# A fused recurrence, MLP and MoE kernel: the triangular products of a superchunk are issued at the end of the one before

## The chip, the cores and the metric

The kernel runs on one core of a Trainium2 chip. The number that counts is the time of one execution in device microseconds (us). Each value of an input is random and in float32; the whole program is one launch.

## The reference

Three layers run one after the other. The first is a recurrence over 768 steps with a 40 x 40 state for each of 4 batches and 8 heads; the second is an MLP with a squared ReLU on the 3072 resulting tokens; the third sends every token to one of 8 experts.

```python
for t in range(S):                                  # B, H, S, D = 4, 8, 768, 40
    y[:, :, t] = einsum('bhd,bhde->bhe', rt, state)
    Sa = einsum('bhde,bhe->bhd', state, at)
    state = state * wt[:, :, None, :] - einsum('bhd,bhe->bhde', Sa, bt) + einsum('bhd,bhe->bhde', vt, kt)
...
x = y, as (3072 tokens) x (8 heads * 40)
h = x @ w_in                                        # 320 -> 2048
x = (max(h, 0) ** 2) @ w_out                        # 2048 -> 320
...
expert = argmax(x @ w_gate)                         # 8 experts, capacity 768 each
y = max(x_e @ w1[e], 0) @ w2[e]                     # 320 -> 1024 -> 320
out = gate_w * y[expert]
```

## The kernel before

**The recurrence.** The 768 steps are cut into NS = 12 superchunks of 64 steps, each of NC = 2 chunks of 32. Within a superchunk the steps are coupled by triangular matrices, one of 32 x 32 for every chunk, head and batch. For superchunk s three methods make and use them. `lower(s, c)`, called for both chunks, issues 64 small matmuls `pa` of the scaled inputs `kb` (in the trace `kb_d`) and `a`, copies one half of the product by ACT into `ab` (two equal copies of it), masks the other half on DVE into `am`, and transposes that into `a` (the name `ak` in the code). `invert(s)` transposes `ab` into `al` on DVE and then inverts all the triangles at once on POOL, by 31 pairs of a multiplication (`tmp`) and a subtraction (`solve_tl`), which both stand at the helper's line L291. `inverted(s)` waits for the last of them, transposes the inverse on DVE (`solve_tf`, L221) and puts it together in `tt` (ACT L224, DVE L225). The solve of the superchunk's first chunk (`psa` on PE, then `sa` on ACT, L332) reads `tt`.

**The rest.** `scale(s)` scales the inputs by running products of the decay (the scans `rq_r` and `rq_q` over `w_d`), `decay(s)` multiplies `a` by the decay (DVE L350), and `step` ends a chunk by the update of the state `zv` (L308); the next superchunk begins with the output `y` (DVE L390), its transposition on PE (`pt`, L456), the decay of `zv` (DVE L350) and the transposition of `zv` (`pz`). The MLP works on the tokens of the preceding superchunk: `pl` products, ReLU and square on ACT and DVE (`g`, L660, split into `gh` and `gl`), `acc` products. Its weights come as doubles and are cut into two float parts at the start: a load on ACT's queue (L514), `Abs` on ACT (L519), four bit operations on DVE (L520 to L523), the high part on ACT (L554 for w_in, into `wi_hi`; L411 for w_out, into `woh`) and the low part by a subtraction, which is on POOL (L528) or on DVE (L530, `lo`). The w_out pieces are `ao0` to `ao15`; the w_in pieces are `a0_0`, `a0_1`, `a0_2` and so on, of which `a0_2` is put into the buffer of `a0_0` (tag "relu", two buffers). `wogl` (L412) are small subtractions for the router.

**What sets the order.** PE's matmuls run in the order in which the program is written (`mm`), and the instructions of an inversion on POOL are chained in their order as well. All else is ordered by a scheduler for each engine, which goes by the program's order, by priorities (higher for s < 2) and by its own estimate of the times. Each engine then runs its list strictly in order. A superchunk is written as seven slots for its first chunk and five for its second, each followed by some pieces of the MLP:

```python
parts = slot_a, slot_b, slot_c, slot_d, slot_e, slot_f, slot_g
if c == 1:
    parts = slot_a, slot_b, slot_d, slot_f, slot_g
```

`slot_a` holds `out` (y) and `right`, `slot_b` the solve, `slot_c` `lower` and `invert` of the next superchunk, `slot_g` the `step`, and in the second chunk `inverted` of the next superchunk behind it.

Of the kernel before, what the change touches and what calls it, by code (L numbers as in the profile page):

```python
# [72 lines left out]
class Rwkv:  # L73
# [101 lines left out]
    def lower(self, s, c):  # L175

        nc = self.nc
        kb, a = self.kb, self.a[s % 2][:, c]
        if c == 0:
            self.ab = self.tile([128, C, 2, NC, H], f"solve.ab{s}", 2)  # L180
        pa = self.psum(f"pa{s}_{c}").rearrange("p (h k s) -> p h k s", h=H, k=2)
        t0 = c * C
        for h, b, i, lane, ty, j in heads():
            rows = BY_COL[j]
            self.mm(pa[lane, h], lhsT=a[rows, j, i], rhs=kb[rows, :, i, t0:t0 + C], start=True, stop=True)
        for u in range(2):
            nc.scalar.copy(self.ab[:, :, u, c, :], pa[:, :, 1, :].rearrange("p h s -> p s h"))
        am = self.tile([128, H, C], f"am.{s}_{c}", 1)
        nc.vector.tensor_tensor(out=am, in0=pa[:, :, 0, :], in1=self.c["mlow"][:, None, :].to_broadcast([128, H, C]),
                                op=ALU.mult)  # L190
        for j in range(2):
            ak = a[BY_STEP[j], j].rearrange("p (h y) t -> p y h t", y=2)
            nc.vector.transpose(out=ak[:, 0], in_=am[BY_STEP[j]])  # L193
            nc.scalar.copy(ak[:, 1], ak[:, 0])

    def invert(self, s):

        nc = self.nc
        al = self.tile([128, C, C], f"solve.al{s}", 2)
        nc.vector.transpose(out=al.rearrange("p s t -> p (s t)"), in_=self.ab.rearrange("p s u c h -> p (s u c h)"))  # L200
        tl = self.tile([128, C, C // 2], f"solve.tl{s}", 2)
# [14 lines left out]
    def inverted(self, s):  # L216

        nc, tl = self.nc, self.tl
        tf = self.tile([128, C, 2, NC, H], f"solve.tf{s}", 2)
# [578 lines left out]
class Moe:  # L798
# [188 lines left out]
    def early(self, rw):  # L987
# [34 lines left out]
        op = [rw.tile([128, 8, 128], f"{t}.op{i}", 2 - i // 2, dt=F32R) for i, t in enumerate(("solve", "solve", "rq16"))]  # L1022
# [332 lines left out]
def tile_rwkv__mlp__moe(ctx, tc, wd, kb, ad, rv, wl, tok, vt, nat, w_in, w_out, w_gate, w1, w2, cap, cst1, cst2, cst3, out):  # L1355
# [9 lines left out]
    with ExitStack() as ph:  # L1365
# [53 lines left out]
        for s in range(NS):  # L1419
# [3 lines left out]
            for c in range(NC):  # L1423
# [7 lines left out]
                def slot_a():  # L1431
                    nonlocal y
                    if s == 0 and c == 0:
                        rw.inverted(0)
                    if last is not None:
                        y = rw.out(*last)
# [13 lines left out]
                def slot_c():  # L1450
                    if s > 1:
                        pieces.append(ml.bursts(s - 1, xs.pop(s - 1)))
                    if more:
                        rw.lower(s + 1, 0)
                        rw.lower(s + 1, 1)
                        rw.invert(s + 1)
# [21 lines left out]
                def slot_g():  # L1478
                    rw.step(s, c, 0)
                    rw.step(s, c, 1)  # L1480
                    if c == 1 and more:
                        rw.inverted(s + 1)

# [137 lines left out]
```

## Time and profile before

| | |
|---|---|
| three runs | 1124.78, 1127.44 and 1131.85 us; median 1127.44 us |
| the profiled execution | 1123.14 us, of which the trace's span is 1121.4 us |
| PE busy | 912.5 us, 81% of the span |
| DVE busy | 851.1 us, 76% |
| ACT busy | 573.1 us, 51% |
| POOL busy | 501.8 us, 45% |

The span falls into three parts. Up to about 226 us the weights are converted beside superchunks 0 and 1, and PE is often idle. From there to about 721 us superchunks 2 to 10 and the MLP run side by side, some 60 us for each. Then follow the last superchunk, the remaining MLP and the experts. A row of the timeline gives the start, the duration, the engine, the line, the operation with what it writes and reads, and in brackets how long the engine was idle before it and which instruction it waited for.

### The profile page before, as it was taken

To read this page: it belongs to the slowest core of one execution; us is meant where nothing else is said; L and a number is where in the kernel's file an instruction comes from. 1 tells how busy PE (TensorE), PEld (TensorE's weight loads), DVE (VectorE), ACT (ScalarE), POOL (GpSimd) and SP (SyncE) were. 2 spreads that over 40 slices of the span, in tenths; PEclk is the share of its full clock that TensorE was granted. 3 is DMA by queue.
4 is the path that set the end of the run, shared out by engine and by line. 5 is a ranking of instruction groups with operands and counts; after the bars stand their busy time and mean duration, and the time that the engine had idled before them with its cause. 6 is when DMAs were issued, how large, how long until landed. Compare 5 with 4: busy or idle time off the path is not lost.

```text
span 1121.4 us, 38788 instructions
## 1 busy us (share of the span) xinstructions
PE 912.5 (81%) x15962; PEld 858.4 (77%) x15962; DVE 851.1 (76%) x1807; ACT 573.1 (51%) x1570; POOL 501.8 (45%) x866
## 2 busy tenths in 40 slices
PE   1645347788798989897979889899899999999992
PEld 1535247687687878796978888899799989999992
DVE  8969887688778788777877888765777967878860
ACT  2425335454454544545545454555474667767750
POOL 4782852828282837465563828270010132223220
PEclk9999998888898989798998889899999998999997
DMA  8823534844353535353434444343195576767720
GB/s 219 251 81 110 147 114 112 267 121 134 104 147 114 151 105 168 90 155 116 135 110 129 133 127 144 91 136 104 39 321 146 163 219 189 229 199 231 216 80 9
DMA packets 86112, 164.19 MB, mean 146 GB/s; under 512 B 15709, under 2 KB 46047, under 8 KB 84960
## 3 DMA queue, kind: packets, MB, share of 16 engines
q1 hardware_dynamic: 76848, 141.52, 43.4%
q10 hardware_dynamic: 6192, 11.06, 3.6%
q0 software_dynamic: 2880, 8.98, 2.4%
q8 instruction: 129, 2.11, 0.8%
q14 instruction: 63, 0.52, 0.2%
HBM read 137.34 MB, written 16.24 MB: 137 GB/s over the span
## 4 chain that ended last, share of the span: by engine, by line
PE 36%; POOL 22%; DVE 16%; issue 9%; DMA 9%; ACT 3%; SPq 1%; POOLq 0%; DVEq 0%; ACTq 0%
POOL tmp L291 11%; POOL solve_tl L291 11%; PE acc L633 8%; PE pl L449 8%; PE upl L449 6%; PE uacc L1143 6%; DMA xg<-x_dram,room 3%; DVE rq_r L126 2%; DMA out_dram<-uo,room 2%; DVE rq_q L139 2%; DVE zv L350 1%; PE pa L294 1%; PE ppq L294 1%; DMA raw<-in_w_in_dram 1%; PE pn L294 1%
## 5 line engine op out<-in xcount | busy, mean ns | idle before, releaser
L291 POOL TENSOR_TENSOR tmp<-solve_al,solve_tl 128x126 f32<-128x126 f32 (+22 forms) x372 | 205.9, 554 | 41.1 <-DVE a L193 12.9
L291 POOL TENSOR_TENSOR solve_tl<-solve_tl,tmp 128x126 f32<-128x126 f32 (+22 forms) x372 | 199.1, 535 | 29.1
L633 PE MATMUL acc<-woh,gh 128*128 128x328 f32 x384 | 130.5, 345 | 1.6 <-ACT x L686 1.6
L449 PE MATMUL pl<-x_hi,wi_hi 128*128 128x256 f32 x384 | 122.2, 318 | 10.0 <-DVE g L660 5.8
L633 PE MATMUL acc<-wol,gh 128*128 128x328 f32 x384 | 123.8, 328 | 0.0
L449 PE MATMUL pl<-x_lo,wi_hi 128*128 128x256 f32 x384 | 115.0, 300 | 7.2 <-DVE x_lo L464 7.2
L660 DVE TENSOR_TENSOR g<-pl,g 128x512 f32<-128x512 f32 x96 | 65.6, 684 | 66.2 <-ACT gh L659 65.9
L449 PE MATMUL pl<-x_hi,wi_lo 128*128 128x256 f32 x384 | 114.9, 299 | 0.0
L291 POOL MEMSET solve_tl<- 128x512 f32 x12 | 6.3, 526 | 214.8 <-DVE solve_al L200 199.1
L1221 POOL DMA_INDIRECT out_dram<-uo,room x30 | 34.3, 1144 | 150.6 <-DVE uo L1210 83.0
L655 ACT ACTIVATE g<-pl 128x512 f32<-128x512 f32 x96 | 57.4, 598 | 76.4 <-PE pl L449 75.2
L633 PE MATMUL acc<-woh,gl 128*128 128x328 f32 x384 | 93.1, 325 | 0.0
L1151 POOL DMA_INDIRECT xg<-x_dram,room x30 | 30.7, 1022 | 139.0 <-DVE room L983 61.4
L449 PEld LDWEIGHTS pl<-x_hi,wi_hi 128*128 128x128 f32 x384 | 78.8, 205 | 14.3 <-DVE g L660 5.9
L449 PEld LDWEIGHTS pl<-x_lo,wi_hi 128*128 128x128 f32 x384 | 79.5, 207 | 7.5 <-DVE x_lo L464 7.5
L1143 PE MATMUL uacc<-w2h,hh 128*128 128x320 f32 x240 | 76.8, 320 | 10.1 <-DVE uo L1210 8.5
L633 PEld LDWEIGHTS acc<-woh,gh 128*128 128x128 f32 x384 | 77.2, 201 | 4.6 <-ACT x L686 1.8
L449 PEld LDWEIGHTS pl<-x_hi,wi_lo 128*128 128x128 f32 x384 | 79.4, 207 | 0.0
L633 PEld LDWEIGHTS acc<-wol,gh 128*128 128x128 f32 x384 | 77.6, 202 | 0.0
L1143 PE MATMUL uacc<-w2h,hl 128*128 128x320 f32 x240 | 75.8, 316 | 0.0
L1143 PE MATMUL uacc<-w2l,hh 128*128 128x320 f32 x240 | 75.5, 315 | 0.0
L661 DVE TENSOR_TENSOR gl<-g,gh 128x512 fp32r<-128x512 f32 x96 | 68.9, 718 | 1.9
(263 smaller groups left out, 2771.5 us busy)
## 6 DMA issues: line engine op xcount, KB each, us to landing
wol<-wol SPq DMA_DIRECT2D x96, 328.0 KB
w<-in_w_dram SPq DMA_DIRECT2D x30, 640.0 KB
w<-in_w_dram SPq DMA_DIRECT2D x30, 512.0 KB
zv<-in_vt_dram SPq DMA_DIRECT2D x48, 208.0 KB
kb_d<-in_kb_dram SPq DMA_DIRECT2D x24, 320.0 KB
zk<-in_tok_dram SPq DMA_DIRECT2D x48, 160.0 KB
rx<-rt SPq DMA_DIRECT2D x192, 40.0 KB
w<-in_w_dram SPq DMA_DIRECT2D x30, 256.0 KB
```

What stands on the lines that cost most here:

```text
L126: nc.vector.tensor_tensor_scan(out=rf[:, ::-1], data0=w[:rows, 1:][:, ::-1], data1=seed, initial=0.0, op0=ALU.mult, op1=ALU.add)
L139: nc.vector.tensor_tensor_scan(out=q.rearrange("p a b -> p (a b)")[:rows], data0=w[:rows, 0:L], data1=seed, initial=0.0, op0=ALU.mult, op1 ...
L291: self.last = f(*a, **k).ins
L294: self.tc.keep_in_program_order(self.nc.tensor.matmul(*a, **k))
L449: tc.keep_in_program_order(tc.nc.tensor.matmul(out, lhsT=a, rhs=b, start=n == 0, stop=n == len(seq) - 1))
L633: self.tc.keep_in_program_order(self.nc.tensor.matmul(*a, **k))
L655: nc.scalar.activation(g, pl, AF.Relu)
L660: nc.vector.tensor_tensor(out=g, in0=pl, in1=g, op=ALU.mult)
L661: self.behind = (square, nc.vector.tensor_tensor(out=gl, in0=g, in1=gh.bitcast(F32), op=ALU.subtract).ins)
L1143: self.tc.keep_in_program_order(self.nc.tensor.matmul(*a, **k))
L1151: nc.gpsimd.indirect_dma_start(out=xg[:, 0:DX], out_offset=None, in_=self.x1, in_offset=bass.IndirectOffsetOnAxis(ap=self.idx[2 * j + t], ...
L1221: self.nc.gpsimd.indirect_dma_start(out=self.out, out_offset=bass.IndirectOffsetOnAxis(ap=self.to[:, n:n + 1], axis=0), in_=o[:, t], in_of ...
```

## The change

It does two things. The copy of `ab` is made once instead of twice (`al` is now transposed from the one copy, read twice), and the buffers that shared the tag "solve" are divided: `ab` and `tl` have a tag with one buffer each, and `al` and `tf` share "solve" with one buffer, where before all four shared two. The expert layer's early buffers are adapted to that. And `lower` and `invert` of superchunk s + 1, which stood in `slot_c` of the first chunk of s, now stand one place earlier: in `slot_g` at the end of the second chunk of s - 1, right behind `inverted(s)`; those of superchunk 1 stand in the first `slot_a`, right behind `inverted(0)`. From L188 of the kernel before on, the lines of the new kernel have a number that is lower by one.

```diff
--- before.py
+++ after.py
@@ -177,14 +177,13 @@
         nc = self.nc
         kb, a = self.kb, self.a[s % 2][:, c]
         if c == 0:
-            self.ab = self.tile([128, C, 2, NC, H], f"solve.ab{s}", 2)
+            self.ab = self.tile([128, C, NC, H], f"ab.{s}", 1)
         pa = self.psum(f"pa{s}_{c}").rearrange("p (h k s) -> p h k s", h=H, k=2)
         t0 = c * C
         for h, b, i, lane, ty, j in heads():
             rows = BY_COL[j]
             self.mm(pa[lane, h], lhsT=a[rows, j, i], rhs=kb[rows, :, i, t0:t0 + C], start=True, stop=True)
-        for u in range(2):
-            nc.scalar.copy(self.ab[:, :, u, c, :], pa[:, :, 1, :].rearrange("p h s -> p s h"))
+        nc.scalar.copy(self.ab[:, :, c, :], pa[:, :, 1, :].rearrange("p h s -> p s h"))
         am = self.tile([128, H, C], f"am.{s}_{c}", 1)
         nc.vector.tensor_tensor(out=am, in0=pa[:, :, 0, :], in1=self.c["mlow"][:, None, :].to_broadcast([128, H, C]),
                                 op=ALU.mult)
@@ -196,9 +195,9 @@
     def invert(self, s):
 
         nc = self.nc
-        al = self.tile([128, C, C], f"solve.al{s}", 2)
-        nc.vector.transpose(out=al.rearrange("p s t -> p (s t)"), in_=self.ab.rearrange("p s u c h -> p (s u c h)"))
-        tl = self.tile([128, C, C // 2], f"solve.tl{s}", 2)
+        al = self.tile([128, C, C], f"solve.al{s}", 1)
+        nc.vector.transpose(out=al.rearrange("p s t -> p (s t)"), in_=self.ab.rearrange("p s c h -> p s (c h)")[:, :, None].to_broadcast([128, C, 2, NC * H]))
+        tl = self.tile([128, C, C // 2], f"tl.{s}", 1)
         tmp = self.tile([128, 144], f"tmp.{s}", 1, tag="am")
         eng, pin = nc.gpsimd, self.pool
         pin(eng.memset, tl, 0.0)
@@ -216,7 +215,7 @@
     def inverted(self, s):
 
         nc, tl = self.nc, self.tl
-        tf = self.tile([128, C, 2, NC, H], f"solve.tf{s}", 2)
+        tf = self.tile([128, C, 2, NC, H], f"solve.tf{s}", 1)
         with self.behind(1):
             nc.vector.transpose(out=tf.rearrange("p t u c h -> p (t u c h)"),
                                 in_=tl[:, :, :, None].to_broadcast([128, C, C // 2, 2]))
@@ -1019,7 +1018,7 @@
         V.tensor_copy(self.mine, slot)
         blk, pos = self.places(slot, "ea")
         nb, n = 2 * FIRST_UNITS, 2 * NE
-        op = [rw.tile([128, 8, 128], f"{t}.op{i}", 2 - i // 2, dt=F32R) for i, t in enumerate(("solve", "solve", "rq16"))]
+        op = [rw.tile([128, m, 128], f"{t}.op{m}", 1, dt=F32R) for t, m in (("solve", 8), ("rq16", 8), ("ab", n - 16))]
         ov = rw.tile([128, n, nb], "rq10.ov", 1, dt=F32R)
         self.experts(end, "ea", 0, FIRST_UNITS)
 
@@ -1432,6 +1431,9 @@
                     nonlocal y
                     if s == 0 and c == 0:
                         rw.inverted(0)
+                        rw.lower(1, 0)
+                        rw.lower(1, 1)
+                        rw.invert(1)
                     if last is not None:
                         y = rw.out(*last)
                     rw.right(s, c)
@@ -1450,10 +1452,6 @@
                 def slot_c():
                     if s > 1:
                         pieces.append(ml.bursts(s - 1, xs.pop(s - 1)))
-                    if more:
-                        rw.lower(s + 1, 0)
-                        rw.lower(s + 1, 1)
-                        rw.invert(s + 1)
 
                 def slot_d():
                     rw.turn(s, c)
@@ -1480,6 +1478,10 @@
                     rw.step(s, c, 1)
                     if c == 1 and more:
                         rw.inverted(s + 1)
+                    if c == 1 and s + 2 < NS:
+                        rw.lower(s + 2, 0)
+                        rw.lower(s + 2, 1)
+                        rw.invert(s + 2)
 
                 parts = slot_a, slot_b, slot_c, slot_d, slot_e, slot_f, slot_g
                 if c == 1:
```

The diff leaves the order on each engine to the scheduler. Three places follow, each as it stands before and then after the change.

DVE in the start-up, around the transposition of the first inverse (`solve_tf0`), before. `ao8` to `ao15` and `lo` are pieces of w_out in conversion, `a0_1` is one of w_in:

```order
L412 TENSOR_TENSOR wogl_97<-pog_964,woh_88 128x8
L530 TENSOR_TENSOR lo15_488<-ao15_481,woh_88 128x320
L520 TENSOR_SCALAR a0_1_506<-a0_1_506 128x256
L221 STREAM_TRANSPOSE solve_tf0_789<-solve_tl0_290 128x1024
L530 TENSOR_TENSOR lo14_477<-ao14_470,woh_88 128x320
L412 TENSOR_TENSOR wogl_97<-pog_978,woh_88 128x8
L521 TENSOR_SCALAR a0_1_506<-a0_1_506 128x256
L520 TENSOR_SCALAR a1_1_526<-a1_1_526 128x256
```

DVE at the same place after the change:

```order
L522 SCALAR_TENSOR_TENSOR ao7_389<-stage_hi_86,ao7_389 128x320
L529 TENSOR_TENSOR lo6_385<-ao6_378,woh_88 128x320
L519 TENSOR_SCALAR ao8_400<-ao8_400 128x320
L220 STREAM_TRANSPOSE solve_tf0_787<-tl_0_288 128x1024
L188 TENSOR_TENSOR am_1_0_827<-pa1_0_793,ct3_106 128x256
L520 TENSOR_SCALAR ao8_400<-ao8_400 128x320
L529 TENSOR_TENSOR lo7_396<-ao7_389,woh_88 128x320
L411 TENSOR_TENSOR wogl_97<-pog_1004,woh_88 128x8
L192 STREAM_TRANSPOSE a1_115<-am_1_0_827 64x8x32 x2
```

The transposition has moved up from the 127th row to the 79th. 49 instructions that stood ahead of it now stand behind it: 31 bit operations of `ao8` to `ao15` (L520 to L523), 8 `lo` subtractions (L530), 9 `wogl` (L412) and the first operation of `a0_1`. Two that stood behind it, the decay of `a` for superchunk 1, now stand ahead of it. Between `solve_tf0` and the first `g` of the MLP (`g0_0`) there are now 222 rows; the first operation of `a0_2` stands 96 rows behind `solve_tf0` and 126 ahead of `g0_0`.

POOL in the start-up, where inversion 0 ends and inversion 1 begins, before:

```order
L291 TENSOR_TENSOR tmp_0_291<-solve_al0_288,solve_tl0_290 128x16
L291 TENSOR_TENSOR solve_tl0_290<-solve_tl0_290,tmp_0_291 128x16
L291 TENSOR_TENSOR zk0_121<-zk0_121,rx_0_0_754 64x2x8x40 x2
L528 TENSOR_TENSOR wi_lo_492<-a0_1_506,wi_hi_491 128x256
L528 TENSOR_TENSOR wi_lo_492<-a0_0_496,wi_hi_491 128x256
L528 TENSOR_TENSOR ml0_544<-a0_2_537,mh0_543 128x256
L291 MEMSET solve_tl1_1168 128x512
L291 COPY solve_tl1_1168<-ct3_106 128x16 x2
L291 TENSOR_TENSOR tmp_1_1169<-solve_al1_1166,solve_tl1_1168 128x31
```

POOL after the change, near the end of inversion 1, 24 of whose 31 pairs have gone by the first `wi_lo`:

```order
L290 TENSOR_TENSOR tmp_1_876<-solve_al1_873,tl_1_875 128x108
L290 TENSOR_TENSOR tl_1_875<-tl_1_875,tmp_1_876 128x9x12
L290 TENSOR_TENSOR tmp_1_876<-solve_al1_873,tl_1_875 128x96
L290 TENSOR_TENSOR tl_1_875<-tl_1_875,tmp_1_876 128x8x12
L527 TENSOR_TENSOR wi_lo_490<-a0_1_504,wi_hi_489 128x256
L290 TENSOR_TENSOR tmp_1_876<-solve_al1_873,tl_1_875 128x91
L527 TENSOR_TENSOR wi_lo_490<-a0_0_494,wi_hi_489 128x256
L290 TENSOR_TENSOR tl_1_875<-tl_1_875,tmp_1_876 128x7x13
L290 TENSOR_TENSOR tmp_1_876<-solve_al1_873,tl_1_875 128x78
```

The subtractions of `a0_1` and `a0_0` stood ahead of inversion 1 and now stand behind 24 of its 31 pairs; that of `a0_2` (`ml0`) now stands behind all of it. On ACT `Abs` of `a0_2`, which needs the buffer of `a0_0`, stands ahead of `sa` of the first solve in both orders, with one or more loads between them.

DVE where superchunk 5 ends and 6 begins (`solve_tf6` is the inverse for superchunk 6, `y_5_1` the output of the last chunk of 5), before:

```order
L308 TENSOR_TENSOR zv0_116<-zv1_117,pn5_1_1_7014 40x4x2x40 x2
L221 STREAM_TRANSPOSE solve_tf6_7033<-solve_tl6_6256 128x1024
L245 STREAM_TRANSPOSE rt_7_1_7707<-rq10_r7_7500 128x8x32
L246 STREAM_TRANSPOSE rt_7_1_7707<-rq10_r7_7500 128x8x8
L139 SCALAR_TENSOR_TENSOR rq10_q7_7710<-wl_7_6979,seed_q_111 128x650
L225 SCALAR_TENSOR_TENSOR tt_6_7035<-solve_tf6_7033,ct3_106,tt_6_7035 128x512
L123 MEMSET seed_q_111 104x16
L660 TENSOR_TENSOR g4_6_7055<-pl4_6_7038,g4_6_7055 128x512
L390 TENSOR_TENSOR y_5_1_7112<-py5_1_7079,qt_5_1_5987 128x320
L126 SCALAR_TENSOR_TENSOR rq16_r8_7717<-w_d_112,seed_q_111 104x1040
L661 TENSOR_TENSOR gl4_6_7058<-g4_6_7055,gh4_6_7057 128x512
L350 TENSOR_TENSOR zv0_116<-zv0_116,g64_6_5793 40x8x2x40 x2
```

DVE after the change, from the sixth row of the same stretch on; ahead of these stand `solve_tf6`, two transpositions `rt`, the decay of `a` and the first `am` of superchunk 7:

```order
L139 SCALAR_TENSOR_TENSOR rq10_q7_7694<-wl_7_6965,seed_q_111 128x650
L224 SCALAR_TENSOR_TENSOR tt_6_7021<-solve_tf6_7019,ct3_106,tt_6_7021 128x512
L192 STREAM_TRANSPOSE a1_115<-am_7_0_7059 64x8x32 x2
L123 MEMSET seed_q_111 104x16
L199 STREAM_TRANSPOSE solve_al7_7105<-ab_7_7024 128x1024
L188 TENSOR_TENSOR am_7_1_7099<-pa7_1_7065,ct3_106 128x256
L126 SCALAR_TENSOR_TENSOR rq16_r8_7701<-w_d_112,seed_q_111 104x1040
L192 STREAM_TRANSPOSE a1_115<-am_7_1_7099 64x8x32 x2
L135 TENSOR_SCALAR rq16_r8_7701<-rq16_r8_7701 104x1040
L659 TENSOR_TENSOR g4_6_7191<-pl4_6_7174,g4_6_7191 128x512
L136 RECIPROCAL seed_q_111<-rq16_r8_7701 104x16
L389 TENSOR_TENSOR y_5_1_7248<-py5_1_7215,qt_5_1_6125 128x320
```

The DVE part of `lower` and `invert` for superchunk 7 (the decay of `a`, `am`, two transpositions each, `solve_al7`) and the scan over `w_d` now stand ahead of `y_5_1`; before, that part stood a dozen rows behind it and the scan right behind it. On PE the 128 `pa` matmuls of superchunk 7 likewise stand ahead of `pt` of `y_5_1`.

## Rows read from the trace of the kernel before

**Rows 1.** Windows: stretch, us; busy us (instructions) of each engine; PE clock, DMA share, GB/s.

```profile
96.00:176.00 80.00, 38.34 (x1036) 32.48 (x1036) 69.11 (x153) 34.88 (x98) 39.23 (x66) 0.99 0.46 123
226.00:721.00 495.00, 427.98 (x9633) 396.74 (x9634) 394.97 (x638) 247.88 (x624) 274.17 (x523) 0.90 0.45 127
```

**Rows 2.** Waits of 200 to 721 us: total us, how often, the longest.

```profile
PE pt L456 <- DVE y L390: 25.1, 10, 3.9
...
DVE solve_tf L221 <- POOL solve_tl L291: 24.6, 9, 7.1
...
PE pz L272 <- DVE zv L350: 17.1, 15, 2.0
```

**Rows 3.** Timeline of PE at the start of superchunk 7.

```profile
528.67 0.60 PE L456 MATMUL pt<-ct,y 128*128 128x128 f32 x3 [3.45 <-DVE y L390]
...
538.09 1.99 PE L294 MATMUL pa<-kb_d,a 40*32 40x64 f32 x128
```

**Rows 4.** Timeline of DVE at the start of superchunk 7.

```profile
523.72 1.25 DVE L221 STREAM_TRANSPOSE solve_tf<-solve_tl 128x1024 f32<-128x1024 f32 x1 [2.48 <-POOL solve_tl L291]
...
539.24 1.40 DVE L350 TENSOR_TENSOR a<-a,g 40x512 f32<-40x512 f32 x2 [0.74 <-PE pa L294]
540.57 0.41 DVE L189 TENSOR_TENSOR am<-pa,ct 128x256 f32<-128x256 f32 x1
...
543.55 0.91 DVE L193 STREAM_TRANSPOSE a<-am 64x256 f32<-64x256 f32 x2
```

**Rows 5.** Timeline of DVE in the start-up.

```profile
72.99 0.28 DVE L520 TENSOR_SCALAR a<-a 128x256 f32<-128x256 f32 x1
84.94 1.25 DVE L221 STREAM_TRANSPOSE solve_tf<-solve_tl 128x1024 f32<-128x1024 f32 x1 [11.67 <-POOL solve_tl L291]
...
175.67 1.29 DVE L660 TENSOR_TENSOR g<-pl,g 128x512 f32<-128x512 f32 x2 [0.71 <-ACT gh L659]
```

**Rows 6.** Groups of DVE by form, 43.5 to 73.3 us: busy us, mean ns, idle before.

```profile
L530 DVE TENSOR_TENSOR lo<-ao,woh 128x320 fp32r<-128x320 f32 x10 | 5.4, 556 | 0.0
L521 DVE TENSOR_SCALAR ao<-ao 128x320 uint32<-128x320 uint32 x8 | 3.7, 485 | 0.0
...
L412 DVE TENSOR_TENSOR wogl<-pog,woh 128x8 fp32r<-128x8 f32 x10 | 1.5, 151 | 0.0
```

**Rows 7.** Timeline of POOL in the start-up (inversions 0 and 1).

```profile
37.33 2.52 POOL L291 TENSOR_TENSOR tmp<-solve_al,solve_tl 128x31 f32<-128x31 f32 x1 [0.90 <-DVE a L193]
...
57.00 1.29 POOL L291 TENSOR_TENSOR solve_tl<-solve_tl,tmp 128x120 f32<-128x120 f32 x1
...
67.67 5.87 POOL L291 TENSOR_TENSOR tmp<-solve_al,solve_tl 128x126 f32<-128x126 f32 x1
...
79.39 0.39 POOL L291 TENSOR_TENSOR solve_tl<-solve_tl,tmp 128x96 f32<-128x96 f32 x1
...
93.85 0.73 POOL L528 TENSOR_TENSOR wi_lo<-a,wi_hi 128x256 fp32r<-128x256 f32 x1 [2.21 <-ACT wi_hi L554]
...
115.86 0.27 POOL L291 TENSOR_TENSOR tmp<-solve_al,solve_tl 128x31 f32<-128x31 f32 x1 [1.44 <-DVE a L193]
...
150.71 0.39 POOL L291 TENSOR_TENSOR solve_tl<-solve_tl,tmp 128x96 f32<-128x96 f32 x1
```

**Rows 8.** Timeline of POOL in the last inversion.

```profile
721.73 0.24 POOL L291 TENSOR_TENSOR tmp<-solve_al,solve_tl 128x31 f32<-128x31 f32 x1 [1.68 <-DVE a L193]
...
732.39 0.95 POOL L291 TENSOR_TENSOR solve_tl<-solve_tl,tmp 128x120 f32<-128x120 f32 x1
...
746.61 0.39 POOL L291 TENSOR_TENSOR solve_tl<-solve_tl,tmp 128x96 f32<-128x96 f32 x1
...
752.26 0.23 POOL L291 TENSOR_TENSOR solve_tl<-solve_tl,tmp 128x16 f32<-128x16 f32 x1
```

**Rows 9.** Timeline of ACT: the first solve.

```profile
100.58 0.42 ACT L332 ACTIVATE sa<-psa 128x320 f32<-128x320 f32 x1
```

**Rows 10.** Timeline of PE: the MLP's third group of products in the start-up.

```profile
176.42 0.58 PE L449 MATMUL pl<-x_hi,wi_hi 128*128 128x256 f32 x1 [5.78 <-DVE g L660]
```

## The prediction

> **What bounds the kernel now.** I read the page's busy shares first, then windows by stage, then the waits, then the timelines at two places. The windows [rows 1] show two different kernels. From 226 to 721 us PE is busy 427.98 of 495 us (86%) and the rest of the engines have room, so there the time is PE's work plus what PE waits at fixed places. From 96 to 176 us PE is busy 38.34 of 80 us while DVE is busy 69.11: the start-up is bound by DVE and by what DVE waits for. In the steady part the waits [rows 2] name the places: PE waits 25.1 us in ten times for `y` ahead of `pt`, and 17.1 us for `zv` ahead of `pz`; DVE, which makes both, waits 24.6 us in nine times for the last subtraction of POOL's inversion ahead of `solve_tf`. So at each start of a superchunk there is one chain: POOL, then DVE (`tf`, ..., `y`, ..., decay of `zv`), then PE. The change lets POOL begin sooner, so it aims at those 24.6 us. What matters is what it puts in their place.
>
> **Superchunks 2 to 10, the wait removed.** POOL's part of an inversion is now started a dozen microseconds sooner, right behind the preceding one, and POOL is busy only 274.17 of 495 us [rows 1]. I take all of the 24.6 us of DVE's waits to go.
>
> **Superchunks 2 to 10, what comes in their place.** In the new order the DVE part of `lower` stands ahead of `y`; before, it stood well behind the decay of `zv`. In superchunk 7 it lasts from 539.24 to 544.46 (543.55 + 0.91), 5.22 us [rows 4]. The long scan over `w_d` moves ahead of `y` as well, but before it stood between `y` and the decay of `zv`, so for `zv` it is neither gain nor loss. Each decay of `zv` therefore comes 5.22 us later by the group and sooner by that boundary's wait: 9 x 5.22 - 24.6 = 22.4 us later in all. Adding the durations in the nine orders one by one gives 4.0 to 5.8 us for a boundary, 36 to 52 for the nine, with 47 for the sum that I take. PE gets something back: the 128 `pa` matmuls, 1.99 us [rows 3], now run ahead of `pt`, in time that PE waits anyhow, and are missing later, where PE is busy: 9 x 1.99 = 17.9. What is left is 22.4 - 17.9 = +4.5 us; the bounds are 36 - 24.6 - 17.9 = -6 and 52 - 24.6 - 17.9 = +10. Within a boundary the wait changes its place: `pt`, which waited 3.45 us in superchunk 7 [rows 3], waits longer, as `y` has both the group and the scan ahead of it, and `pz` hardly waits, since the decay follows `y` directly.
>
> **The start-up, DVE.** `solve_tf0` stands 49 rows further up. DVE ended the last instruction ahead of it at 73.27 and waited 11.67 us for POOL, to 84.94 [rows 5]. The 49 rows are 31 bit operations at 0.485, 8 `lo` at 0.556, 9 `wogl` at 0.151 and one of 0.28 [rows 5, 6]: 21.1 us, less 0.07 each by which neighbours overlap (539.24 + 1.40 against 540.57 [rows 4]), so 17.7. The decay of `a`, 1.40, comes ahead. DVE arrives at 73.27 - 17.7 + 1.4 = 57.0 and stands still until POOL ends inversion 0, with those 49 instructions queued behind it.
>
> **The start-up, POOL.** At 57.00 POOL begins its second 128x120 subtraction [rows 7]. The last inversion went from that instruction to its end in 752.26 + 0.23 - 732.39 = 20.1 us [rows 8]; here it took 27.9, to 84.94. The difference is in single instructions: a 128x126 multiplication takes 5.87 us at 67.67 [rows 7], while DVE is busy with conversions. With DVE idle I take the last inversion's tempo, and `solve_tf0` starts at 77.1; with the old tempo it stays at 84.94 and everything below is 7.8 us later. The Trainium skill (SBUF — State Buffer, Who interferes with whom) has a rule for it: a DVE instruction with two SBUF inputs contends with a GpSimd instruction that reads SBUF, over ports that the two share. The 5.87 us agree with it, the times by the rule are those with 77.1, and without it those with 84.94.
>
> **The start-up, the new wait.** In POOL's new order the subtractions `wi_lo` of `a0_1` and `a0_0`, done about 94.6 before (93.85 + 0.73 [rows 7]), stand behind 24 pairs of inversion 1. That inversion gets `al` about 6 us behind `solve_tf0` and so begins its pairs near 85.4, not 115.86. The 24 pairs took 151.10 - 115.86 = 35.2 us in inversion 1, 42.5 in inversion 0 [rows 7] and 25.3 in the last [rows 8]. DVE is busy beside it, as in inversion 1, so I take 35.2, and 2 us for the two subtractions and the pair's half between them: `a0_0` is free at about 122.5 (112.7 to 129.9). On ACT `Abs` of `a0_2` needs that buffer. Behind it, in ACT's strict order, stand loads of raw weights and `sa` of the first solve, which went at 100.58 before [rows 9]; now it goes at about 123.3. DVE reaches its own first operation on `a0_2` some 38.7 us behind `solve_tf0` (96 rows), at 115.8, and waits too.
>
> **The start-up, how much reaches PE.** The next place where PE visibly waits for DVE is `g0_0`, 175.67 on DVE [rows 5] and 5.78 us of waiting on PE [rows 10]. By DVE's queue: 126 rows from `a0_2` to `g0_0`, whose own durations add up to 59.6 (at the window's mean of 69.11/153 = 0.45 they would be 57), and some 6 us of idle time, of the 10.9 (80 - 69.11) that DVE had in the window [rows 1]: 123.1 + 59.6 + 6 = 188.7. By the first solve: from `sa` to `g0_0` it was 175.67 - 100.58 = 75.1 us; with all the idle time kept `g0_0` is at 198.4, with none at 187.5. I take 191.5, +16. PE has then done `pa` of superchunk 2 (1.99), which stood behind before: +14. As PE is nearly full from there on, a delay here isn't made good later. The low end is DVE's queue without the wait: 77.1 + 98.3 (222 rows) = 175.4, less the 2 of `pa`, -2. The high end has the old tempo of POOL (+7.8) and half of the slower 24 pairs (+3.6): +25.
>
> **Parts at nothing.** One copy of `ab` instead of two saves ACT twice a copy per superchunk; ACT is busy 247.88 of 495 us [rows 1] and `pa` waits for nothing of it. The split of the buffers keeps as many of each tile as the new order uses at a time; `tf` shares its buffer with `al`, and `al` comes behind `tt` anyhow. The last superchunk has no `lower` behind its inverse, so nothing changes there.
>
> **Sum.** 1123.14 (the profiled execution) + 14 + 4.5 = 1141.6. The profiled execution lies 4.3 under the median of 1127.44, so in terms of the median 1146.
>
> **Rivals.**
> The stall stays in the start-up: POOL's late `wi_lo` is made good, because other conversions fill DVE's queue and `sa` isn't what PE waits for at 176 us. Then 1127.4 - 2 + 4.5 = 1130. For it: the queue alone gives 175.4, and PE idles over half of that window. Against it: both queues are strict, and ACT's wait lies ahead of the first solve itself. 0.17.
> No effect at all, as POOL's place in the queue isn't what bounds: PE's work is unchanged, what it waits less at one place it waits more at another, about 1127. 0.08. The Trainium skill (Perfetto Trace Analysis, Identifying the Most-Contended Engine) says to optimise the engine with the highest occupancy first, and POOL with 45% is the lowest; by that alone the time would be this one.
> Faster: the group on DVE costs `y` nothing, because DVE does it in time in which it is idle, 495 - 394.97 = 100 us of the stretch [rows 1], of which POOL's waits are 24.6. Then these 24.6 go and nothing takes their place: 1127.4 - 24.6 = 1103 without a start-up loss, 1117 with it. It decides at 28.5/9 = 3.2 us (24.6 + 17.9 - 14 over nine): if `zv` is put off by less than that for a boundary by the group, the change pays. Against it stands DVE's strict order, with the group's 5.22 us between `tf` and `y`. 0.09.
> Worse start-up: the old tempo on POOL and the late `sa` together, 1127.4 + 25 + 10 = 1162. 0.14.
>
> **How the numbers follow.** The forecast, 1137 to 1156, has 0.52; its likeliest time is 1146. To hold 8 in 10 I leave out most of the faster case and the end of the worst one: 1123 to 1164. Below 1127.4 by over 1%, which is about what a measurement of this kernel can tell from no change, lies only the faster case: 0.09. Within 1% (to 1138.7) lie the hidden stall, the case without effect and a little of the forecast's lower end: 0.28. Slower by more: 0.63.
>
> **What would show it.** In the changed kernel's trace: DVE idle for some 20 us ahead of the first `tf`, which starts near 77; `wi_lo` of w_in on POOL only near 122, with an idle ACT ahead of `Abs` of `a0_2`; the first `sa` near 123, the first `g` near 190. From superchunk 2 on: no wait of `tf` for POOL, about 5 us more between `tf` and `y`, `pt` waiting 4 to 7 us for `y` and `pz` next to nothing; a period near 61 us. I am wrong on the start-up if `sa` is early or the first `g` lies near 175; wrong on the boundaries if the sum of the waits ahead of `pt` and `pz` falls by more than it takes in `pa`; and wrong on POOL if the first `tf` stays near 85.

## The result, and the profile after

The changed kernel is slower by 0.81%: 1136.05 us against 1127.03 (medians of 18 runs each), ratio 1.0081 with a 95% interval of 1.0054 to 1.0108. That is +9.1 us (6.1 to 12.2) where +18.5 was forecast: the sign was right and the size twice too large. The profiled execution took 1136.11 us (span 1134.3); that of before, 1123.14, lay 3.9 under its median, so the two traces differ by 12.9 and show some 4 us too much.

Windows of the changed kernel, the same stretches and columns as [rows 1]:

```profile
96.00:176.00 80.00, 42.08 (x986) 35.60 (x987) 74.90 (x173) 36.55 (x107) 29.58 (x56) 0.91 0.52 141
226.00:721.00 495.00, 419.24 (x9339) 390.76 (x9330) 376.48 (x616) 234.47 (x584) 300.57 (x520) 0.89 0.46 126
```

In the steady stretch PE gets through 9339 matmuls in 495 us, before through 9633. The waits of 200 to 721 us, as in [rows 2]:

```profile
PE pt L455 <- DVE y L389: 30.9, 7, 6.8
...
PE pr L293 <- issue: 6.9, 3, 3.3
PE pa L293 <- issue: 4.8, 4, 1.6
PE pz L271 <- DVE zv L349: 4.7, 6, 2.3
PE pl L448 <- issue: 4.4, 3, 2.5
DVE rt L244 <- DMA zv<-in_vt_dram: 3.5, 3, 1.6
...
PE acc L632 <- issue: 2.0, 1, 2.0
```

No row of `tf` waiting for POOL is left: the 24.6 us are gone, as intended. `pt` waits 30.9 instead of 25.1 and `pz` 4.7 instead of 17.1. Two kinds of row are new. `rt`, right behind `tf`, waits for transfers, 9.1 us in eight waits. And PE stands still for 18.1 us in all (6.9 + 4.8 + 4.4 + 2.0) with "issue", which means that no wait explains it.

DVE at the start of superchunk 7, two rows of the kernel before that [rows 4] leaves out, and then the changed kernel:

```profile
528.13 0.48 DVE L390 TENSOR_TENSOR y<-py,qt 128x320 f32<-128x320 f32 x1
...
531.46 1.67 DVE L350 TENSOR_TENSOR zv<-zv,g 40x640 f32<-40x640 f32 x2
```

```profile
529.00 1.23 DVE L220 STREAM_TRANSPOSE solve_tf<-tl 128x1024 f32<-128x1024 f32 x1
...
531.84 0.45 DVE L244 STREAM_TRANSPOSE rt<-rq_r 128x256 f32<-128x256 f32 x1 [1.61 <-DMA zv<-in_vt_dram]
...
539.33 2.30 DVE L126 TENSOR_TENSOR_SCAN rq_r<-w_d,seed_q 104x1040 f32<-104x1040 f32 x1
541.55 0.46 DVE L389 TENSOR_TENSOR y<-py,qt 128x320 f32<-128x320 f32 x1
...
542.76 1.63 DVE L349 TENSOR_TENSOR zv<-zv,g 40x640 f32<-40x640 f32 x2
```

`tf` begins without a wait. `y` now begins 12.55 us behind it (541.55 - 529.00), before 4.41 (528.13 - 523.72); the decay of `zv` 13.76 us, before 7.74. On PE `pt` then waits 6.79 us where it waited 3.45 [rows 3]:

```profile
542.16 0.87 PE L455 MATMUL pt<-ct,y 128*128 128x128 f32 x3 [6.79 <-DVE y L389]
```

The start-up, on DVE, POOL and ACT:

```profile
49.91 1.25 DVE L158 TENSOR_TENSOR kb_d<-kb_d,rq_r 104x1024 f32<-104x1024 f32 x1 [6.12 <-DMA kb_d<-in_kb_dram]
...
51.49 1.28 POOL L290 TENSOR_TENSOR tl<-tl,tmp 128x120 f32<-128x120 f32 x1
...
76.14 1.25 DVE L220 STREAM_TRANSPOSE solve_tf<-tl 128x1024 f32<-128x1024 f32 x1 [6.78 <-POOL tl L290]
...
118.83 0.72 POOL L527 TENSOR_TENSOR wi_lo<-a,wi_hi 128x256 fp32r<-128x256 f32 x1
...
119.58 0.43 ACT L518 ACTIVATE a<-raw 128x256 f32<-128x256 f32 x1 [1.83 <-POOL wi_lo L527]
...
120.47 0.44 ACT L331 ACTIVATE sa<-psa 128x320 f32<-128x320 f32 x1 [0.47 <-issue]
...
183.50 0.69 DVE L659 TENSOR_TENSOR g<-pl,g 128x512 f32<-128x512 f32 x1
```

The first `tf` is at 76.14 (forecast 77.1), the second `wi_lo` at 118.83 (122.5), the first `sa` at 120.47 (123.3, before 100.58 [rows 9]): the chain was there as described. But `g0_0` is at 183.50, not 191.5.

### The profile page after: what moved, and what is told of

Its sections match the earlier page's. It is cut to its first block, busy times and chain, and to the rows that moved or that the text cites. A ratio compares the mean times of both kernels' runs of the same rounds, so it can differ in the third digit from the quotient of the medians.

```text
span 1134.3 us, 38764 instructions
## 1 busy us (share of the span) xinstructions
PE 912.2 (80%) x15962; PEld 859.1 (76%) x15962; DVE 847.1 (75%) x1807; ACT 567.5 (50%) x1546; POOL 525.1 (46%) x866
## 4 chain that ended last, share of the span: by engine, by line
PE 48%; DVE 18%; DMA 11%; issue 7%; POOL 7%; ACT 4%; SPq 1%; POOLq 0%; ACTq 0%; DVEq 0%
PE pl L448 13%; PE acc L632 12%; PE uacc L1142 6%; PE upl L448 6%; DMA out_dram<-uo,room 3%; PE ppq L293 3%; POOL tmp L290 3%; POOL tl L290 3%; DVE rq_r L126 3%; DMA xg<-x_dram,room 2%; PE pn L293 2%; DVE rq_q L139 2%; DMA zk<-in_tok_dram 1%; DMA rx<-rt 1%; ACT zv L334 1%
## 5 line engine op out<-in xcount | busy, mean ns | idle before, releaser
L290 POOL TENSOR_TENSOR tmp<-solve_al,tl 128x126 f32<-128x126 f32 (+22 forms) x372 | 202.7, 545 | 132.8 <-DVE a L192 104.6
L290 POOL TENSOR_TENSOR tl<-tl,tmp 128x126 f32<-128x126 f32 (+22 forms) x372 | 224.4, 603 | 29.1
L448 PE MATMUL pl<-x_hi,wi_hi 128*128 128x256 f32 x384 | 122.5, 319 | 5.4 <-issue 2.5
L1220 POOL DMA_INDIRECT out_dram<-uo,room x30 | 33.9, 1130 | 150.0 <-DVE uo L1209 84.0
L293 PE MATMUL pa<-kb_d,a 40*32 40x64 f32 x1536 | 30.6, 241 | 58.3 <-DVE a L283 52.6
L293 PEld LDWEIGHTS pa<-kb_d,a 40*32 40x32 f32 x1536 | 27.5, 123 | 59.9 <-DVE a L283 52.8
```

What stands on the lines that cost most here:

```text
L290: self.last = f(*a, **k).ins
L293: self.tc.keep_in_program_order(self.nc.tensor.matmul(*a, **k))
L448: tc.keep_in_program_order(tc.nc.tensor.matmul(out, lhsT=a, rhs=b, start=n == 0, stop=n == len(seq) - 1))
L1220: self.nc.gpsimd.indirect_dma_start(out=self.out, out_offset=bass.IndirectOffsetOnAxis(ap=self.to[:, n:n + 1], axis=0), in_=o[:, t], in_of ...
```

## The experiments

Ratios are against the kernel before in the same session, with 95% intervals.

**Which part costs.** Three kernels divide the change. `start_only` moves superchunk 1's triangles alone, `bound_only` the others alone, `buffers_only` none:

```diff
 start_only:   slot_g: -  lower/invert(s + 2)      slot_c: +  if more and s > 0: lower/invert(s + 1)
 bound_only:   slot_a: -  lower/invert(1)          slot_c: +  if s == 0: lower/invert(s + 1)
 buffers_only: both -                              slot_c: +  if more: lower/invert(s + 1)
```

> The changed kernel with only the triangles of superchunk 1 moved (behind the first inverse); those of 2 to 11 stay in slot_c. By the two traces the start-up is worth +3 to +5 us: 1130 to 1132 against 1127, first tf near 76, first sa near 120, first g near 183. By the forecast's terms it is +14: 1141, first g near 191. If only the moves at the boundaries cost something: 1127.

> The changed kernel with superchunk 1's triangles left in slot_c and those of 2 to 11 moved to the end of the superchunk before. By the two traces the boundaries are worth +9 to +12 us: 1136 to 1139. By the forecast's terms +4.5: 1131.5. If the start-up makes all of the difference: 1127.

> The changed kernel's buffers and its single copy, with no triangles moved. Forecast and traces: 1127, within 0.5% of the kernel before. If the shared buffer of al and tf or the single buffer of ab costs a wait at each superchunk: 1130 to 1140, with tf or al waiting for a reader of the shared buffer.

Measured: `buffers_only` 0.9972 (0.9948 to 0.9995), `start_only` 1.0006 (0.9981 to 1.0030), `bound_only` 1.0079 (1.0047 to 1.0110). On a base of 1124 us the buffers and the single copy bring 3 us, the start-up costs 1.0006 - 0.9972 = 0.0034, or 3.8 us, and the boundaries cost 1.0079 - 0.9972 = 0.0107, or 12.0 us, each to about 4. Together the three parts make 12.7 us, at the upper end of what the whole change measures (6.1 to 12.2). The start-up's +14 and the boundaries' +4.5 were both mis-sized, against each other.

**Why the start-up cost so little.** `start_dve` is `start_only` with nothing of the conversion behind inversion 1 on POOL:

```diff
-POOLED_IN = (0,)
+POOLED_IN = ()
```

> As start_only (superchunk 1's triangles moved, the others not), with the subtractions of the first w_in piece on DVE instead of POOL, so that nothing of the conversion stands behind inversion 1. If the wait of the conversion for POOL is what delays the first sa from 100.6 to 120.3, sa goes near 103 and the time falls by the 4 us that start_only took over buffers_only. If the 49 conversions that wait with DVE for POOL delay the router's matmuls and with them psa, which stands behind them on PE, sa goes near 115 and the time stays within 3 us of start_only.

Measured: 1.0019 (0.9996 to 1.0042), the same as `start_only`. In its trace `sa` is at 119.16, near neither of the two times expected (103 and 115). PE's and ACT's timelines:

```profile
107.90 1.55 PE L632 MATMUL pog<-wg,wt 128*128 128x8 f32 x6 [2.78 <-DVE wogl L411]
...
114.86 1.29 PE L293 MATMUL psa<-rh,tt 32*32 32x40 f32 x64
```

```profile
117.43 0.44 ACT L518 ACTIVATE a<-raw 128x256 f32<-128x256 f32 x1 [1.40 <-DVE wi_lo L529]
...
119.16 0.44 ACT L331 ACTIVATE sa<-psa 128x320 f32<-128x320 f32 x1 [0.24 <-issue]
```

`psa` stands in PE's program order behind the router's matmuls `pog`, and these need the w_out pieces whose conversion waited with DVE for POOL. In the changed kernel `psa` is at 114.73, too, and in the kernel before it was at 98.34: that is 16.4 of the 20 us by which `sa` is late. The rest stands in ACT's own queue. There `start_dve` only exchanges a wait for POOL by one for DVE, so that `sa` comes 1.2 us sooner than in `start_only` (120.32), and this changes no time that shows.

**What DVE work ahead of `y` costs.** `burden` is the kernel before with a useless reduction between `tt` and `y`:

```diff
+        with self.tc.issue_after(i):            # i: the last step of tt
+            i = self.nc.vector.tensor_reduce(out=tf[:, 0:512], in_=<tl, each value 10 times>, axis=AX.X, op=ALU.max).ins
...
+        with self.tc.issue_after(self.load) if c == 1 and self.load is not None else ExitStack():
             self.nc.vector.tensor_mul(y..., py, ...)
```

> The kernel before, with one DVE instruction more in each of ten superchunks, between tt and y: a reduction over 128x5120 numbers, about 5.3 us, whose result nothing reads. It prices DVE work ahead of y alone: no pa, no POOL work and no buffer is moved. If DVE work ahead of y costs its full length, as the forecast had it: +45 to +53 us (1169 to 1177). If DVE's idle time takes it up: under +10 (1124 to 1134).

Measured: 1.0449 (1.0412 to 1.0487), +50 us. The group of the added line and the wait that answers to [rows 2]:

```profile
L236 DVE TENSOR_REDUCE solve_tf<-solve_tl 128x512 f32<-128x5120 f32 x10 | 54.7, 5474 | 0.0
```

```profile
PE pt L467 <- DVE y L401: 61.5, 9, 11.0
```

54.7 us of DVE work cost 50: nine tenths of its length, though DVE is idle a fifth of that stretch before and is not full with it either (busy 405.06 of 495 us). The price that the forecast put on work ahead of `y` holds. No run puts the same reduction behind `y`, so how much of the price comes from its place isn't shown by itself.

**The group behind `y`.** `slot_b` is the kernel before with `lower` and `invert` moved from `slot_c` to the end of `slot_b`; `slot_a` has the new buffers and puts them behind `right` in `slot_a`, with the decay of `zv` drawn ahead of them:

```diff
 slot_b:  in slot_b  +  if c == 0 and more: lower/invert(s + 1)             (behind others(0))
 slot_a:  in slot_a  +  if c == 0 and s > 0: next(decay); if more: lower/invert(s + 1)   (behind right)
```

> The kernel before, its buffers too, with lower and invert at the end of slot_b instead of slot_c: three pieces of the MLP sooner, but on DVE still behind y and the decay of zv. If what costs time in the change is that the group passes y, this takes most of the 24.6 us of waits for POOL and pays little for them: 1103 to 1117, waits of tf for POOL under 8 us. If PE's work bounds and every wait removed comes up elsewhere: 1125 to 1129.

> The changed kernel's buffers, with the triangles of superchunks 2 to 11 behind y and the decay of zv in slot_a: as early as they can be without passing y on DVE, with pa right behind py and pr on PE. If passing y is what costs: at least as good as slot_b, 1105 to 1117. If pa next to other small matmuls is what costs (pauses of PE without a wait): the pauses are as long as in the changed kernel, 15 to 20 us, and the time is 1122 to 1135.

Measured: `slot_b` 0.9914 (0.9882 to 0.9946), some 10 us faster than before and 19 faster than the changed kernel. `slot_a` 1.0031 (1.0009 to 1.0053): a miss for the theory that only passing `y` costs. Waits of `slot_b`, then of `slot_a`:

```profile
PE pt L456 <- DVE y L390: 12.3, 9, 3.5
...
DVE solve_tf L221 <- POOL solve_tl L291: 7.6, 2, 4.7
```

```profile
PE pz L271 <- DVE am L188: 35.0, 8, 5.8
```

In `slot_b` the wait for POOL falls from 24.6 to 7.6 us, and `pt`'s with it (25.1 to 12.3). In `slot_a` `y` is as early, but `pz` waits 35.0 us for `am`, which it doesn't read. `am` is the last reader of the PSUM tile of `pa`, and all these products take turns in four such tiles, so `pz` seems to wait for its tile. That is read from trace and code; no run here gave it a fifth.

**The wait of `rt`.** `rt3` is the changed kernel with a third buffer for `rt`; in `rt3_held` `rt` must besides stay behind `tf`, so that the order is the old one; `before_rt3` has only the third buffer:

```diff
-            self.rt[s, c] = self.by_step(r, 1 + c * C, f"rt.{s}_{c}", 2)
+            self.rt[s, c] = self.by_step(r, 1 + c * C, f"rt.{s}_{c}", 3)     # rt3_held: for c == 1 behind tf
```

> The changed kernel with a third buffer for rt. In its trace rt, right behind tf, waits some 1.1 us per superchunk for a transfer that still reads the buffer, and holds up the two scans and y behind it. With the third buffer, rt and both scans stand ahead of tf in DVE's order and y comes some 5 us sooner. If the wait and the work ahead of y are what the boundaries cost: 1136 - 20 to - 35, so 1101 to 1116. If the pauses of PE that no wait explains (19.6 us in the changed kernel, 3.3 before) are the cost: they stay, and the time is 1130 to 1136.

> The changed kernel with a third buffer for rt, but with rt held behind tf, so that DVE's order at the start of a superchunk stays that of the changed kernel: the group and both scans ahead of y, without the wait for the buffer. It parts what the third buffer brought (about 15 us): if the wait of 9.1 us over nine superchunks was it, the time is 1117 to 1128 against 1136; if it was the two scans and rt, which then moved ahead of tf, it stays at 1131 to 1137.

> The kernel before with only the third buffer for rt. Its scans and rt then stand ahead of tf, in the time in which DVE waits for POOL, and y and the decay of zv come sooner by 2 to 4 us a superchunk. If work between tf and y costs its length there too: 1095 to 1112 against 1123. If POOL's inversion, which begins no sooner, keeps the period: 1118 to 1125, with longer waits of tf for POOL.

Measured: `rt3` 0.9945 (0.9911 to 0.9978), `rt3_held` 1.0058 (1.0034 to 1.0082), `before_rt3` 0.9969 (0.9948 to 0.9990). With the third buffer no row of `rt` waiting for a transfer is left, in `rt3_held` neither. Taking away the wait alone is worth 0.2%, within what these runs can tell; taking the two scans and `rt` out of the stretch between `tf` and `y` as well is worth 1.4%. A window of `rt3`, and its waits at `pt`:

```profile
226.00:721.00 495.00, 429.62 (x9855) 398.70 (x9856) 396.39 (x649) 250.77 (x623) 318.52 (x563) 0.94 0.47 132
```

```profile
PE pt L455 <- DVE y L389: 15.7, 5, 4.7
```

9855 matmuls against 9339, at a granted clock of 0.94 against 0.89: in this trace PE spends less of the stretch at the lower of its two levels, and it has fewer and shorter waits at `pt` (15.7 us against 30.9). How much of the gain the clock is stays open: over the whole execution the granted clock was 0.952 here (1113.78 us), and other executions of `rt3` at 0.895 to 0.902 took 1108.77 to 1116.80 us. In the kernel before the same buffer brings 0.3% only. There `tf` waits for POOL as long as ever, since `lower` begins no sooner:

```profile
DVE solve_tf L221 <- POOL solve_tl L291: 24.7, 9, 6.1
```

**PE's pauses.** `kb_late` delays the load of the next `kb`, which begins when `pa` has read the old one:

```diff
+        if s > 2:
+            with self.tc.issue_after(self.solved):      # sa of the latest solve, on ACT
+                nc.scalar.copy(kb[BY_COL[0], 0, 0, 0:1], self.c["lim"][BY_COL[0], 0:1])
+                nc.scalar.copy(kb[BY_COL[1], 0, 0, 0:1], self.c["lim"][BY_COL[1], 0:1])
         for j in range(2):
             nc.sync.dma_start(out=kb[BY_COL[j]], in_=src["kb"][s, j])
```

> The changed kernel with two ACT copies of one column into kb behind sa of each superchunk's first solve, so that the 640 KB load of the next kb begins only after it and not right behind pa. The pauses of PE without a wait in the changed kernel (19.6 us) each begin at a packet of the queue that carries instructions; if the burst of loads at the same time delays these packets, the pauses fall to under 8 us. If the pauses come from the many small matmuls in a row alone, they stay at 15 to 20. If they were what the boundaries cost, the time falls by as much, to about 1125; if PE would wait for y there anyhow, it stays within 1133 to 1137.

Measured: 1.0081 (1.0049 to 1.0112), no different from the changed kernel. Its waits:

```profile
PE pt L459 <- DVE y L393: 38.8, 8, 6.1
...
PE pr L297 <- issue: 5.3, 6, 1.9
PE pa L297 <- issue: 3.3, 4, 1.7
```

With two smaller rows (1.0 and 0.5) the pauses are 10.1 us, between the two sums that were expected; in the changed kernel they are 18.1, and in the other five traces with the moved boundaries 15.5 to 19.5. `pt`'s wait for `y` grows from 30.9 to 38.8, by as much as they fall. So the burst of loads lengthens the pauses, and the pauses cost nothing that the time shows: PE only gets sooner to a wait for DVE. `bound_rt3`, one of the two fastest kernels below, has 19.5 us of them.

**The parts together.** Five kernels combine what gained: the place (`slot_b`) with new buffers (`slot_b_new`), with the third `rt` buffer (`slot_b_old_rt3`), with both (`slot_b_rt3`); and the moved boundaries with the third `rt` buffer and the old start-up (`bound_rt3`), with superchunk 2 left in place as well (`late_rt3`).

> The candidate for the best: the changed kernel's buffers, the triangles of the next superchunk at the end of slot_b, and a third buffer for rt. By the sum of the parts, 0.9914 for the place, 0.997 for the buffers and what the third buffer brings to the kernel before (unknown, 0.98 to 1.0): 1090 to 1112. If the parts take the same waits: as slot_b, 1110 to 1116.

> slot_b with the changed kernel's buffers and single copy, without the third rt buffer. If place and buffers add: 0.988 to 0.991, 1111 to 1115. If the new buffers cancel the gain of the place: 1.000 or more, 1124 and over; then the loss of slot_b_rt3 is theirs and not the third buffer's.

> slot_b with the old buffers and the third rt buffer. If y and zv so early bring nothing because PE then waits at pa for banks of PSUM (13.8 us ahead of pa in slot_b_rt3 against 0 in slot_b): 1.000 to 1.004, 1124 to 1129. If the third buffer is harmless there: 0.988 to 0.992, 1111 to 1116.

> bound_only (start-up as before, triangles of 2 to 11 moved) with the third rt buffer. If the work between tf and y is what the boundaries cost, as in the step from the changed kernel to rt3 (minus 15 us): 1134 - 15 = 1119, and with the start-up's 4 us saved against rt3 1112 to 1116. If rt3's gain came with its start-up: 1125 to 1134.

> As bound_rt3, with superchunk 2's triangles also left in their old place, so that only 3 to 11 are moved. In the two first traces the boundaries of superchunks 2 and 3 lost some 4 us where the forecast gave them a gain of 5. If leaving superchunk 2 alone takes half of that back: 2 to 4 us under bound_rt3. If not, the same within 2 us.

Measured: `slot_b_rt3` 1.0035 (1.0014 to 1.0056), `slot_b_new` 0.9919 (0.9894 to 0.9944), `slot_b_old_rt3` 1.0006 (0.9984 to 1.0028), `bound_rt3` 0.9907 (0.9883 to 0.9931), `late_rt3` 0.9920 (0.9893 to 0.9948). Place and third buffer, each a gain alone, cancel, against what was expected of `slot_b_rt3` (1116 or less); the new buffers add nothing that shows to the place (`slot_b_new`). Waits of `slot_b_old_rt3`, of which `slot_b` has 2.5 us at `pa` and none at the other two:

```profile
PE pa L294 <- ACT zk L404: 15.7, 8, 2.0
...
PE pr L294 <- DVE zv L308: 7.7, 21, 0.6
PE psa L294 <- DVE tt L225: 7.6, 8, 2.5
```

`y` and `zv` come so early there that `pt` and `pz` hardly wait, and PE stops a step further on, at `pa`, `psa` and `pr`. Why that is more than was saved isn't settled by these rows. With the moved boundaries the same buffer pays in full: `bound_rt3` is 1.7% better than `bound_only`. The best of all, `bound_rt3` and `slot_b`, are equal and 0.9% faster than the kernel before. Leaving superchunk 2's triangles in place brought nothing, but it doesn't give that boundary back either: in `late_rt3` `tf` of superchunk 2 still waits 5.2 us for POOL, and the group of superchunk 3 stands ahead of the `y` behind it.

## Why the prediction was right or wrong

Two terms of the sum failed: "how much reaches PE" in the start-up, +14, which measures 3.8, and the +4.5 of the boundaries, which measures 12.0. Their errors have opposite signs. That the time still lay inside 1123 to 1164 is in part luck.

**The wait removed.** Right that POOL's waits at `tf` all go. Where the boundaries' sum went wrong is read from the second solves of superchunks 1, 3 and 10. PE's timeline, before, and then after:

```profile
201.47 1.12 PE L294 MATMUL psa<-rh,tt 32*32 32x40 f32 x64
...
323.37 1.12 PE L294 MATMUL psa<-rh,tt 32*32 32x40 f32 x64
...
739.11 1.12 PE L294 MATMUL psa<-rh,tt 32*32 32x40 f32 x64
```

```profile
205.30 1.12 PE L293 MATMUL psa<-rh,tt 32*32 32x40 f32 x64
...
326.96 1.12 PE L293 MATMUL psa<-rh,tt 32*32 32x40 f32 x64
...
754.01 1.12 PE L293 MATMUL psa<-rh,tt 32*32 32x40 f32 x64
```

The changed kernel is behind by 3.8, 3.6 and 14.9 us. At the seven boundaries of superchunks 4 to 10, whose waits were 1.2 to 2.5 us each and 12.7 together, the forecast's terms make 7 x (5.22 - 1.99) - 12.7 = +9.9, and the traces grow by 11.3; their period, (754.01 - 326.96) / 7 = 61.0 us, is the one foretold. At the two long waits, superchunks 2 and 3 with 11.9 us together, the terms make 2 x (5.22 - 1.99) - 11.9 = -5.4, and the traces change by -0.2. The trace of `bound_only` has +8.3 and -2.4 for the same stretches. So most of what the forecast missed at the boundaries is the gain that it took from the two long waits.

**What comes in their place.** It is at superchunk 2 that this gain is lost: at its second solve the changed kernel is 6.1 us behind (265.96 - 259.89), so that it loses 2.3 there, where the terms make a gain of 3.9, and gains 2.5 at superchunk 3, where they make 1.5. DVE at the start of superchunk 2, before, and then after:

```profile
225.66 1.25 DVE L221 STREAM_TRANSPOSE solve_tf<-solve_tl 128x1024 f32<-128x1024 f32 x1 [7.14 <-POOL solve_tl L291]
...
229.29 1.67 DVE L350 TENSOR_TENSOR zv<-zv,g 40x640 f32<-40x640 f32 x2
```

```profile
221.43 1.23 DVE L220 STREAM_TRANSPOSE solve_tf<-tl 128x1024 f32<-128x1024 f32 x1
...
231.34 0.45 DVE L244 STREAM_TRANSPOSE rt<-rq_r 128x256 f32<-128x256 f32 x1 [1.83 <-DMA w_d<-in_wd_dram]
...
235.03 2.35 DVE L126 TENSOR_TENSOR_SCAN rq_r<-w_d,seed_q 104x1040 f32<-104x1040 f32 x1 [0.70 <-DMA w_d<-in_wd_dram]
...
237.54 1.75 DVE L349 TENSOR_TENSOR zv<-zv,g 40x640 f32<-40x640 f32 x2
```

Before, `rt` and both scans stood behind the decay of `zv` at this boundary, and the decay began 3.63 us behind `tf`. Now they stand ahead of it, together with the group, and it begins 16.11 us behind `tf`. It is put off by 12.5 us, not by the 5.22 that was read at superchunk 7, and not by 4.0 to 5.8 as the forecast had it for every boundary; that the scan is "neither gain nor loss" for `zv` doesn't hold here. Over the nine boundaries of the two traces the decay begins 62.2 us later behind `tf`, not 47. By the forecast's other terms that would be 62.2 - 24.6 - 17.9 = +19.7; the 12.0 measured lie some 1 us a boundary below, and no run shows where PE got that back. PE's granted clock in this stretch, 0.89 against 0.90 [rows 1], is a part that isn't separated either.

**The group ahead of `y`.** The price held (`burden`, nine tenths of its length), and with the group behind `y` (`slot_b`) the sign turns. `slot_a`, with the group behind `y` too, is 0.3% slower, so the place on DVE isn't all that counts. What the step didn't see is what POOL's wait had covered, the wait of `rt` for its buffer, 1.61 us in superchunk 7; the runs give it little of the time (`rt3_held`). The gain by `pa` in PE's waiting time was counted in full; the pauses at just that place take some of it, but nothing that the time shows (`kb_late`).

**The start-up.** The times of the chain came out within 4 us at each link up to `sa`. The first of them, `tf` at 76.14, was right by two errors that cancel, which is luck: POOL was at its second 128x120 subtraction at 51.49 and not at 57.00, and took 24.6 us from there and not 20.1; DVE came only at 69.36 (76.14 - 6.78) and not at 57.0, since it waited 6.12 us for a load, among others, on the way. So the tempo of POOL beside an idle DVE, and with it the rule of the Trainium skill (SBUF — State Buffer, Who interferes with whom), was hardly put to the test. The term that failed is "how much reaches PE". `g0_0` came 8.0 us sooner than forecast: 2.8 by `sa`, and 5.2 since from `sa` to `g0_0` it took 183.50 - 120.47 = 63.0 us and not 191.5 - 123.3 = 68.2. DVE kept little of the idle time that I left it (busy 74.90 of 80 us), and the group of superchunk 1 was already done. And of the 7.8 us by which `g0_0` is later than before, the start-up has only 3.0. The first `g` of `start_only` and of `bound_only`:

```profile
178.69 0.69 DVE L659 TENSOR_TENSOR g<-pl,g 128x512 f32<-128x512 f32 x1 [0.75 <-ACT gh L658]
```

```profile
180.81 0.69 DVE L659 TENSOR_TENSOR g<-pl,g 128x512 f32<-128x512 f32 x1 [0.70 <-ACT gh L658]
```

The 3.0 us of `start_only` fit the 3.8 of its time: for them the sentence holds that a delay there isn't made good later. The 5.1 us of `bound_only` come with the triangles of superchunk 2, whose group now stands ahead of `g0_0` on DVE; they are made good by the second solve of superchunk 1 (201.15 against 201.47). The new wait of ACT for POOL was real, 1.83 us, but it is a small part of what makes `sa` late: most is `psa`, behind the router's matmuls.

**The parts at nothing.** The buffers and the single copy bring 0.3%, at the edge of what these runs tell.

**The rivals.** "The stall stays in the start-up" came nearest (1130 by its sum, which lacked the boundaries' 7.5 us more). "No effect" is excluded. "Faster" named a condition that nearly all runs bear out, that `zv` be put off by less than 3.2 us a boundary. Counted from `tf`, the changed kernel puts it off by 6.9 us and `rt3_held` by 5.9, and both are slower; `bound_rt3` by 2.1 and `slot_b` by 0.2, and both are faster. `slot_a`, with 0.2, is the exception.

## What to carry to other kernels

When a wait is removed from a strict queue, look first at what now stands ahead of the consumer: a useless reduction there cost nine tenths of its length, while `lower` and `invert`, moved to a place behind the consumer, made the kernel 0.9% faster. Read the new order at every boundary that is summed, the ones with the longest waits above all: superchunk 7 stood for nine here, and at superchunk 2 the delay was 12.5 us and not 5.2. Gains that were measured apart need not add: two that brought 0.3% and 0.9% alone came to nothing together.

## What the runs showed of the hardware

PE's pauses. In the changed kernel's trace PE stops without a wait eleven times from 200 to 721 us, for 0.28 to 3.31 us, most often in the middle of a row of like matmuls. Each of the eleven ends 1.2 to 1.6 us after the end of a packet on the queue q8, of kind "instruction"; 79 packets of that queue fall into the stretch. That PE waits for instructions there is concluded from this alone. One of the pauses, PE's timeline and the transfers of the same 3.2 us:

```profile
354.08 0.57 PE L293 MATMUL pr<-zv,a 104*32 104x40 f32 x39 [3.31 <-issue]
```

```profile
q1 hardware_dynamic: 187, 0.54, 64.7%
q8 instruction: 1, 0.02, 2.5%
```

The kernel before has 3.5 us of such rows from 200 to 721 us, the changed one 18.1: the 128 matmuls of `pa` now stand close to the other small ones, and the loads that `pa` sets free fall into the same time. Of these two only the loads were varied (`kb_late`: 10.1 us). The Trainium skill (Runtime: NRT & Kernel Launch, Instruction fetch mechanics) says that instructions come in blocks of 16 KiB by the engine's own DMA queue, mostly hidden. The packets agree (79 carry 1.29 MB), and most pass without a pause; at these eleven the fetch isn't hidden.
